# Casting keys, queries and weights inside GpSimd's loads: linear attention with a SiLU feed-forward on one core

## The chip, the core and the metric

The kernel runs on one core of one Trainium2 chip. The metric is device time in microseconds (us); every number called "time" is the median of all executions of that series, slow ones included. An execution over 1.5% above the fastest of the same kernel is called slow, and ratios use fast executions alone. A profile is one execution taken by the hardware profiler; its span is about 2 us shorter than the time of that execution.

Engines: TensorE (PE in profiles; PEld is its weight load), VectorE (DVE), ScalarE (ACT), GpSimd (POOL) and SyncE (SP). SP, GpSimd and ScalarE can issue DMAs. Each engine works through its instructions in order. An instruction that waits holds up all behind it.

## The reference

Decayed linear attention for 4 batches of 8 heads, 768 positions and head size 64, then a feed-forward layer with SiLU, all float32.

```python
for b in range(nb):                                   # blocks of 64 positions
    intra = einsum('bhic,bhjc->bhij', qb, kb) * Dmask # lam ** (i - j), lower triangle
    intra = einsum('bhij,bhjd->bhid', intra, vb)
    inter = einsum('bhid,bhde->bhie', qb * lam_pow, kv_state)
    out[:, :, sl] = intra + inter
    kv_state = lam_block * kv_state + einsum('bhsd,bhse->bhde', kb * rev_pow, vb)
x = out.transpose(0, 2, 1, 3).reshape(3072, 512)
h = x @ w_in                                          # 512 x 2048
return (h * sigmoid(h)) @ w_out                       # 2048 x 512
```

Both kernels write each decay as a product of a power of lam that belongs to the query and one that belongs to the key or value, so the state needs no rescaling.

## The kernel before

All work is a list of operations with durations. A planner in the kernel file puts them into one order, which fixes each engine's order before anything runs. There are 24 chunks of 128 positions. For a chunk, keys and values are loaded as float32, keys are cast to bf16 into a block-diagonal tile (two heads on 128 partitions), that tile is transposed (by TensorE for chunks 0 to 7, by a DMA from SP after that), values are scaled by GpSimd and copied by VectorE into a block-diagonal tile, and queries are scaled by GpSimd. TensorE fills the time between attention steps with feed-forward matmuls of earlier chunks.

The parts that the argument touches (cuts marked `# ...`):

```python
def load_q(b, j):                       # 256 positions, float32, rows of 512 bytes, by SP
    # ...
    nc.sync.dma_start(out=t.tile, in_=q[b, :, 256 * j:256 * j + 256, :].rearrange("h (s t) d -> s h t d", t=2))

def load_seg(src, tag, b, c0, n):       # one piece per head, float32 rows of 256 bytes, by SP
    for hh in range(8):
        # ...
        nc.sync.dma_start(out=t.tile[64 * two:64 * two + 64, :, p, :], in_=r)

def load_w(which, i, n):                # float32 into a staging tile "wt", then a cast
    # ...
    nc.sync.dma_start(out=t.tile.rearrange("p (a b) -> p a b", b=sh[2]), in_=src)
    # ... nc.scalar.activation(dst_j, src_j, AF.Copy)  or  nc.vector.tensor_copy(dst_j, src_j)

def prep_q(b, j, head):                 # decay of queries; chunks from 4 on: GpSimd
    eng = nc.gpsimd if e == "POOL" else nc.vector
    eng.tensor_tensor(tb.tile[:, sl], tf.tile..., tabq[...], op=AL.mult)
    # ... then a transpose by TensorE, or nc.sync.dma_start_transpose

def prep_k(c, src, src_ops, coff, head):
    for h in range(2):
        nc.vector.tensor_copy(kb.tile[hs, :, :, h, :], i)     # float32 -> bf16, block-diagonal
    # ... then a transpose by TensorE (c < 8), or nc.sync.dma_start_transpose

def prep_v(c, src, src_ops, coff, head):
    eng = nc.gpsimd if e == "POOL" else nc.vector
    eng.tensor_tensor(tv.tile, i, t[...].to_broadcast([128, 2, NP, D]), op=AL.mult)
    for h in range(2):
        nc.vector.tensor_copy(vb.tile[hs, :, :, h, :], tv.tile[hs])
```

Rings: two staging tiles each for queries, keys and values, three block-diagonal key tiles, five weight staging tiles. SP issues everything (loads, transposes and stores) except one load of 4 KB.

## Time and profile before

The time was 252.43 us (251.91 to 252.95). The span falls into three stretches:

| stretch, us | TensorE busy, us | what it is |
|---|---|---|
| 0 to 50 | 42.6 of 50 | filling: weights and first chunks arrive, partly matmuls on zeros |
| 50 to 190 | 117.1 of 140 | mixed: attention chunks with feed-forward between |
| 190 to 249 | 55.2 of 59 | dense: the feed-forward of the last eight chunks |

First the page of the kernel before: busy time of the engines, three rows of the map in 40 slices (tenths busy; PEclk is the granted TensorE clock), the chain of work that ended last by engine and by line, and two groups of instructions (line, engine, operation, output <- input, count, busy us, mean ns of one, idle us of the engine ahead of them and what ended most of it).

```profile
span 248.8 us, 4537 instructions
...
PE 214.9 (86%) x1781; PEld 126.3 (51%) x1781; DVE 108.5 (44%) x197; ACT 119.4 (48%) x230; POOL 52.7 (21%) x58
...
PE   6679899969599699566999896995899999999994
...
PEclk9999999997889999997999999999999999999999
DMA  5999999544698998699767989979442001210022
...
PE 48%; DMA 19%; SPq 15%; DVE 9%; issue 3%; POOL 2%; ACT 2%; POOLq 0%; DVEq 0%; ACTq 0%
PE h L633 22%; PE o L656 19%; SPq L303 10%; DMA qf<-in_q_dram 8%; DVE vbd L475 5%; DMA vf<-in_v_dram 3%; DMA wt<-in_moe_w_in_dram 3%; PE op L565 3%; DMA kfh<-in_k_dram 2%; DMA qT<-qb 2%; PE kv L737 2%; DVE sbd L601 1%; POOL vs L468 1%; DMA kf<-in_k_dram 1%; DVE ss L542 1%
...
L468 POOL TENSOR_TENSOR vs<-vf,tab 128x512 bf16<-128x512 f32 x20 | 20.8, 1062 | 86.4 <-DMA vf<-in_v_dram 68.1
L475 DVE COPY vbd<-vs 64x512 bf16<-64x512 bf16 x48 | 29.6, 617 | 19.5 <-POOL vs L468 18.8
...
```

TensorE is busy for 86% of the span, and the map shows the gaps in the middle. SP's issuing makes 15% of the chain ("SPq"). GpSimd's value scaling (L468) sat idle 68.1 us waiting for values to land. The value copy (L475) takes 617 ns in the mean, and stands with 5% in the chain.

The same copy with its spread of durations, from the view of that tile:

```profile
...
L475 DVE COPY vbd<-vs x48: 275/291/2007, 11.6 to 178.1; 64x512 bf16<-64x512 bf16 x48
...
```

A median of 291 ns and a longest of 2007 ns show two kinds of execution: alone, and while something blocks it. Next, who TensorE waited for (total us, times, longest):

```profile
...
PE kv L585 <- POOL vs L468: 8.9, 5, 2.7
PE kv L585 <- DVE sbd L601: 8.8, 5, 3.3
PE sc L536 <- DMA kT<-kbd: 3.0, 1, 3.0
...
PE sc L536 <- DMA qT<-qb: 1.7, 2, 1.1
...
```

The state update ("kv") waits for scaled values and for VectorE's state copies, 8.9 and 8.8 us. Last, the mixed stretch by windows (busy us and instructions in brackets of each engine; then granted clock, mean busy share of the DMA engines, GB/s):

```profile
...
core 0: us, PE busy (x) PEld busy (x) DVE busy (x) ACT busy (x) POOL busy (x), PEclk, DMA share, GB/s
...
50.00:190.00 140.00, 117.13 (x1117) 68.44 (x1114) 78.80 (x140) 63.89 (x131) 37.93 (x29) 0.96 0.82 175
...
```

### The profile page before, as it was taken

Reading aid. Unit: us, or ns where it says so; the run is one execution under the profiler, and the core shown is the slowest. Engines: PE = TensorE matmul, PEld = TensorE weight load, DVE = VectorE, ACT = ScalarE, POOL = GpSimd, SP = SyncE. Lnnn points to the kernel's source line nnn. Section 1 sums busy time; section 2 is a strip of 40 time slices with the busy share of each in tenths; the row PEclk is TensorE's granted clock in tenths of the full one; section 3 lists DMA queues with packets and bytes.
Section 4 is the critical chain, followed back from the end, with each engine's and each line's share of the span. In section 5 each row is a group of like instructions: output and inputs, shape, how many; then the busy total and the mean of one; then the engine's idle time right before and its main releaser. Section 6 shows DMA issues by size and latency. Waiting matters only on the chain.

```text
span 248.8 us, 4537 instructions
## 1 busy us (share of the span) xinstructions
PE 214.9 (86%) x1781; PEld 126.3 (51%) x1781; DVE 108.5 (44%) x197; ACT 119.4 (48%) x230; POOL 52.7 (21%) x58
## 2 busy tenths in 40 slices
PE   6679899969599699566999896995899999999994
PEld 4477776735397386322455352443454444444441
DVE  4884852447286846594177247255740000000000
ACT  2369776723166287421685233654434751177310
POOL 7802100330320910180061005504300000000000
PEclk9999999997889999997999999999999999999999
DMA  5999999544698998699767989979442001210022
GB/s 143 243 281 251 358 383 328 140 125 91 178 243 190 251 216 154 127 285 211 148 161 162 167 192 237 217 156 191 80 122 84 0 0 45 84 42 0 5 82 84
DMA packets 94885, 40.15 MB, mean 161 GB/s; under 512 B 69264, under 2 KB 89744, under 8 KB 94864
## 3 DMA queue, kind: packets, MB, share of 16 engines
q1 hardware_dynamic: 94720, 39.86, 68.1%
q8 instruction: 14, 0.23, 0.4%
q14 instruction: 7, 0.06, 0.1%
q10 hardware_dynamic: 144, 0.00, 0.0%
HBM read 27.27 MB, written 6.29 MB: 135 GB/s over the span
## 4 chain that ended last, share of the span: by engine, by line
PE 48%; DMA 19%; SPq 15%; DVE 9%; issue 3%; POOL 2%; ACT 2%; POOLq 0%; DVEq 0%; ACTq 0%
PE h L633 22%; PE o L656 19%; SPq L303 10%; DMA qf<-in_q_dram 8%; DVE vbd L475 5%; DMA vf<-in_v_dram 3%; DMA wt<-in_moe_w_in_dram 3%; PE op L565 3%; DMA kfh<-in_k_dram 2%; DMA qT<-qb 2%; PE kv L737 2%; DVE sbd L601 1%; POOL vs L468 1%; DMA kf<-in_k_dram 1%; DVE ss L542 1%
## 5 line engine op out<-in xcount | busy, mean ns | idle before, releaser
L633 PE MATMUL h<-x,w_in_bf 128*128 128x256 bf16 (+1 forms) x512 | 92.8, 333 | 0.4 <-ACT g L640 0.4
L656 PE MATMUL o<-w_out_bf,g 128*128 128x512 bf16 x384 | 90.3, 383 | 0.0
L640 ACT ACTIVATE g<-h 128x256 bf16<-128x256 f32 (+1 forms) x128 | 62.0, 490 | 35.8 <-PE h L633 34.0
L633 PEld LDWEIGHTS <-w_in_bf 128*128 128x128 bf16 x512 | 48.9, 99 | 32.9 <-issue 2.2
L656 PEld LDWEIGHTS <-g 128*128 128x128 bf16 x384 | 35.7, 99 | 37.3 <-issue 1.1
L468 POOL TENSOR_TENSOR vs<-vf,tab 128x512 bf16<-128x512 f32 x20 | 20.8, 1062 | 86.4 <-DMA vf<-in_v_dram 68.1
L475 DVE COPY vbd<-vs 64x512 bf16<-64x512 bf16 x48 | 29.6, 617 | 19.5 <-POOL vs L468 18.8
L666 ACT ACTIVATE ob<-o 128x512 f32<-128x512 f32 x24 | 14.3, 597 | 44.6 <-PE o L656 43.5
L371 POOL TENSOR_TENSOR qb<-qf,tab 128x1024 bf16<-128x1024 f32 (+1 forms) x12 | 22.3, 1856 | 34.5 <-DMA qf<-in_q_dram 34.4
L585 PE MATMUL kv<-vs,kbd 128*128 128x64 bf16 x176 | 12.1, 196 | 17.9 <-POOL vs L468 8.9
L599 ACT ACTIVATE sbd<-kv 64x256 bf16<-64x256 f32 x42 | 15.8, 376 | 23.5 <-PE kv L585 18.9
L424 DVE CAST kbd<-kf 64x512 bf16<-64x512 f32 x40 | 19.4, 486 | 16.1 <-DMA kf<-in_k_dram 15.3
L585 PEld LDWEIGHTS <-kbd 128*128 128x128 bf16 x176 | 10.2, 100 | 26.3 <-issue 16.9
L542 DVE TENSOR_TENSOR ss<-sc,mask 128x512 bf16<-128x512 f32 x20 | 13.8, 691 | 16.0 <-PE sc L536 15.6
L601 DVE CAST sbd<-kv 64x256 bf16<-64x256 f32 x38 | 16.0, 422 | 7.9 <-PE kv L585 3.4
L565 PE MATMUL op<-ss,vbd 128*128 128x64 bf16 (+1 forms) x192 | 15.3, 198 | 1.3 <-DVE ss L542 1.0
L615 ACT ACTIVATE x<-op 128x512 bf16<-128x512 f32 x16 | 11.9, 746 | 8.5 <-PE op L565 8.4
L737 PE MATMUL kv<-zt 128*128 128x256 bf16 x69 | 11.3, 319 | 3.7 <-ACT sbd L599 2.1
L565 PE MATMUL op<-qT,sbd 128*128 128x64 bf16 (+1 forms) x160 | 14.4, 196 | 0.0
L565 PEld LDWEIGHTS <-vbd 128*128 128x128 bf16 x192 | 12.8, 99 | 2.5 <-DVE vbd L475 0.6
L565 PEld LDWEIGHTS <-sbd 128*128 128x128 bf16 x160 | 11.5, 99 | 2.7 <-issue 1.3
L536 PE MATMUL sc<-qT,kT 128*128 128x64 bf16 x160 | 7.9, 193 | 4.7 <-DMA kT<-kbd 3.0
(52 smaller groups left out, 94.5 us busy)
## 6 DMA issues: line engine op xcount, KB each, us to landing
qf<-in_q_dram SPq DMA_DIRECT2D x12, 512.0 KB, 5.2
out_dram<-ob SPq DMA_DIRECT2D x24, 256.0 KB, 2.4
wt<-in_moe_w_in_dram SPq DMA_DIRECT2D x8, 512.0 KB, 7.0
wt<-in_moe_w_out_dram SPq DMA_DIRECT2D x4, 1024.0 KB, 10.0
kf<-in_k_dram SPq DMA_DIRECT2D x32, 96.0 KB, 3.0
vf<-in_v_dram SPq DMA_DIRECT2D x32, 96.0 KB, 2.8
kfh<-in_k_dram SPq DMA_DIRECT2D x8, 128.0 KB, 5.6
vfh<-in_v_dram SPq DMA_DIRECT2D x8, 128.0 KB, 5.6
```

The source lines that it names most:

```text
L303: nc.sync.dma_start(out=t.tile[64 * two:64 * two + 64, :, p, :], in_=r)
L371: eng.tensor_tensor(tb.tile[:, sl], tf.tile.rearrange("p h s d -> p s h d")[:, sl], tabq[:, j, sl, :, None].to_broadcast([128, 2 // nn, H, ...
L424: nc.vector.tensor_copy(kb.tile[hs, :, :, h, :], i)
L468: eng.tensor_tensor(tv.tile, i, t[:, :, :, None].to_broadcast([128, 2, NP, D]), op=AL.mult)
L475: nc.vector.tensor_copy(vb.tile[hs, :, :, h, :], tv.tile[hs])
L542: nc.vector.tensor_tensor(sb.tile.rearrange("a s p b -> a (s p) b"), ps.tile.rearrange("a s p b -> a (s p) b"), mask1[:, None].rearrange(" ...
L565: nc.tensor.matmul(o_cols(p, sub), lhsT=l, rhs=r, start=not ovs["started"], stop=i == len(steps) - 1, skip_group_check=True)
L585: nc.tensor.matmul(kvp.tile[:, p, :], lhsT=kb.tile[:, s, p, :, :], rhs=tv.tile[:, s, p, :], start=st, stop=True, skip_group_check=True)
L601: nc.vector.tensor_copy(nb.tile[hs, :, h, :], kvp.tile[hs])
L633: nc.tensor.matmul(hb.tile, lhsT=w_in_bf[:, ko, m * 128:(m + 1) * 128], rhs=xt[g].tile[:, ko, :], start=(ko == 0), stop=(ko == 3))
L640: nc.scalar.activation(gb.tile, hb.tile, AF.Silu)
L656: nc.tensor.matmul(po.tile, lhsT=gts[g, m][0].tile[:, mt * C:(mt + 1) * C], rhs=w_out_bf[:, m, :], start=(m == 0), stop=(m == 15))
```

## The change

The intent is to take the conversion from float32 to bf16 off the compute engines. A DMA issued by GpSimd can cast on its way, so keys (all but those of the first chunk), queries and weights go straight into their final bf16 tiles. The queries' decay is applied when the attention output is copied out of PSUM, where a copy was needed anyway. GpSimd no longer scales anything. It issues loads.

```diff
-GROUPS = [2, 2, 2, 2, 4, 4, 4, 4]
-NHEAD = 4
+GROUPS = [2, 2, 2, 2, 2, 2, 4, 4, 4]
+NHEAD = 2
+NSP = 2
# ... planner: other constants, separate queues, limits for descriptors
-    SLOTS = {"qf": 2, "qb": 2, "qT": 3, "kf": 2, "vf": 2, ..., "kbd": 3, "kT": 3, ..., "ob": 3, "wt": 5, ...}
+    SLOTS = {"qb": 5, "qT": 4, "big": 3, ..., "kseg": 4, "kT": 4, ..., "ob": 7, ...}
# ... queries
-            nc.sync.dma_start(out=t.tile, in_=q[b, :, 256 * j:256 * j + 256, :].rearrange("h (s t) d -> s h t d", t=2))
+            nc.gpsimd.dma_start(out=t.tile[:, jj], in_=q[b, :, C * blk:C * blk + C, :].rearrange("h s d -> s h d"))
# ... keys: eight pieces of a segment, cast into the block-diagonal tile
+                nc.gpsimd.dma_start(out=t.tile[hs, 0:n, p, two, :],
+                                    in_=k[b, hh, 64 * c0:64 * (c0 + n), :].rearrange("(c s) d -> s c d", s=64))
-                    nc.vector.tensor_copy(kb.tile[hs, :, :, h, :], i)
# ... values stay float32; the first two segments from SP, the rest from GpSimd
+                QS[eng].dma_start(out=t.tile[hs, :, p, :], in_=v[b, hh, ...])
# ... weights
-            nc.sync.dma_start(out=t.tile.rearrange("p (a b) -> p a b", b=sh[2]), in_=src)
+        o = load(lambda: nc.gpsimd.dma_start(out=dst, in_=src), ...)
# ... value scaling: VectorE only
-        a = add(f, [("POOL", pool_ns(512))] + ([("DVE", dve_ns(512))] if head else []), ...)
+        a = add(f, ("DVE", dve_ns(512)), ...)
# ... output copy: VectorE only, with the queries' decay
-            if e == "ACT":
-                nc.scalar.activation(dst, ob.tile, AF.Copy)
-            else:
-                nc.vector.tensor_copy(dst, ob.tile)
+            nc.vector.tensor_tensor(xt[g].tile[:, :, C * off:C * off + C], ob.tile, tabo[:, :, C * blk:C * blk + C], op=AL.mult)
```

The planner runs again on the new list, so the order of all engines changes too.

## The prediction

> **What bounds it now.** The profiled span is 248.8 us, in three stretches (busy time by windows):
>
> - 0-20 us, filling: the first FFN matmul starts at 19.8 us (timeline).
> - 20-190 us, mixed: TensorE is busy 145.1 of 170 us. In the view of waits the state update waits 8.9 us for GpSimd's value scaling and 8.8 us for VectorE's state copies; scores wait 4.7 us for transposing DMAs. Granted clock falls to 0.83 in 50-70 and 110-120, badly fed windows.
> - 190-249 us, dense: two FFN groups, four blocks of 64 matmuls at 13.81 us. The change shortens nothing here.
>
> Two causes stand behind the mixed stretch. First, one queue issues every load: in the chain of waits SP issues take 15%, about 0.62 us each, back to back from 49.7 to 76 us; GpSimd's idle time before value scaling is 68 us, waiting for values. Second, VectorE and GpSimd block each other: the value copy takes 275 ns at least, 291 median, 2007 at most, 29.6 us for 48. At the median that would be 14, so an estimated 15.6 us is blocking. The Trainium skill, "SBUF — State Buffer", section "Who interferes with whom", describes an exclusive lock on the shared port; these durations agree.
>
> **What changes.**
>
> - Removed: key casts 24.5 us (VectorE 22.6), weight casts 13.3 us, query scaling 22.3 us and value scaling 21.8 us on GpSimd, the blocking, the weight staging ring.
> - Added to VectorE: value scaling, about 16 us; all 24 output copies with a multiply at about 0.7 us (the mask multiply takes 691 ns), +11 us, while ScalarE loses 11.9; about 9 us of zeroing. VectorE stays near 105 us: not the bound.
> - Moved: issue splits over two queues. GpSimd gets roughly 130 DMAs; at an assumed 0.7-1 us each, 90-130 us. Prefetch deepens (key ring 2 to 4, values 2 to 3, queries 2 to 5 buffers).
> - DMA: reads stay float32. Query rows go from 512 to 256 bytes, 12 thousand packets more on 95 thousand. DMA share is 71% in 50-80 and 66% in 160-190: room there. 0-50 us is saturated (97-100%) and gains little.
>
> **Sum.** First FFN matmul 3 us earlier (no table or multiply ahead of the first scores, a head of two chunks). Of some 23 us of idle TensorE in 50-190, 13 go. Steadier feeding saves 2 us of lowered clock. New waits give back 1. About 17 us of 252.4: **235 us**, range 226 to 245. Faster by over 2%: 0.88; within 2%: 0.08; slower: 0.04.
>
> **What would show it.** Value copies all near 0.29 us; no wait of the state update on GpSimd; SP under 5% of the chain; TensorE busy above 90%; first FFN matmul at 15-18 us; dense blocks still 13.8 us. If VectorE's busy time passes 120 us, or its output copy or value scaling is what TensorE waits for, the moved work was mis-sized.
>
> **What would make it wrong.** The skill, same page, section "SBUF: two separate sides", says GpSimd can't write descriptors while VectorE runs a two-port copy; no run here shows it yet. If a GpSimd issue costs 1.5 us or more, its in-order queue becomes the new single issuer and the gain falls under 6 us. Casting DMAs could move data more slowly than plain ones and delay weights (all needed by about 46 us) and values. A lower granted clock under denser TensorE work would also eat gain.

## The result and the profile after

The time after is 237.44 us (237.16 to 237.73), against 252.43 us before. The ratio is 0.941, with a 95% interval of 0.931 to 0.950. A ratio is the mean time of one kernel's fast runs over that of the other's of the same rounds, so it isn't quite the ratio of the medians quoted. On another chip, with more runs, the same kernel came to 0.934.

The page after, lines that answer those above:

```profile
span 235.3 us, 4708 instructions
...
PE 213.5 (91%) x1871; PEld 133.3 (57%) x1871; DVE 94.3 (40%) x209; ACT 112.0 (48%) x248; POOL 105.9 (45%) x161
...
PE   6699579999999958996999949999999999999993
...
PEclk9999959999999999999999976999999999999999
DMA  7999799796999999999999999999920002100022
...
PE 48%; DMA 36%; POOL 12%; issue 2%; ACT 0%; POOLq 0%; SPq 0%; ACTq 0%
...
L503 DVE COPY vbd<-vs 64x512 bf16<-64x512 bf16 x48 | 16.4, 342 | 0.6
...
```

TensorE is busy for 91% of a span that is 13.5 us shorter. SP's issuing has gone from the chain. In its place stand DMAs with 36% and GpSimd's issuing with 12%. The DMA row reads 9 from about 59 to 170 us, where before it had gaps. Value copies fell from 29.6 to 16.4 us in total, though not all to 0.29 us as predicted (the longest takes 0.67):

```profile
...
L503 DVE COPY vbd<-vs x48: 273/290/669, 9.2 to 177.3; 64x512 bf16<-64x512 bf16 x48
...
```

TensorE's waits and the mixed stretch:

```profile
...
PE sc L557 <- DMA kT<-kseg: 8.9, 5, 3.4
PE kv L605 <- DVE sbd L619: 2.1, 1, 2.1
...
```

```profile
...
50.00:190.00 140.00, 130.77 (x1242) 81.19 (x1239) 58.38 (x114) 70.69 (x165) 74.02 (x107) 0.98 1.37 145
...
```

The 8.9 us for scaled values are gone and the 8.8 us for state copies are 2.1. A new one has come: scores wait 8.9 us for transposing DMAs of keys, which before was 3.0 us. From issue to landing such a transpose took a median of 3.5 us before and 9.5 us after. In all, TensorE's idle time in 50 to 190 us went from 22.9 to 9.2 us. Those 13.6 us are about the whole 13.5 us by which the span fell. The rest nearly cancels: TensorE's idle time in the first 50 us grew from 7.4 to 8.9 us, and its busy time fell from 214.9 to 213.5. The fill didn't shorten (first feed-forward matmul at 19.75 us before, 19.46 after), and blocks of 64 dense matmuls still take 13.81 us.

### The profile page after: what moved, and what is told of

Its sections match the earlier page's. It is cut to its first block, busy times and chain, and to the rows that moved or that the text cites. A ratio compares the mean times of both kernels' runs of the same rounds, so it can differ in the third digit from the quotient of the medians.

```text
span 235.3 us, 4708 instructions
## 1 busy us (share of the span) xinstructions
PE 213.5 (91%) x1871; PEld 133.3 (57%) x1871; DVE 94.3 (40%) x209; ACT 112.0 (48%) x248; POOL 105.9 (45%) x161
## 3 DMA queue, kind: packets, MB, share of 16 engines
q0 software_dynamic: 57056, 15.08, 73.5%
## 4 chain that ended last, share of the span: by engine, by line
PE 48%; DMA 36%; POOL 12%; issue 2%; ACT 0%; POOLq 0%; SPq 0%; ACTq 0%
PE h L652 22%; PE o L678 21%; DMA kT<-kseg 18%; DMA qb<-in_q_dram 15%; DMA kseg<-in_k_dram 3%; POOL kseg L369 3%; POOL qb L312 2%; PE op L585 2%; POOL big L384 2%; POOL w_in_bf L397 2%; PE sc L557 1%; PE kv L605 1%; POOL w_out_bf L397 1%; POOL kbh L344 1%; ACT ob L688 0%
## 5 line engine op out<-in xcount | busy, mean ns | idle before, releaser
L369 POOL DMA_DIRECT2D kseg<-in_k_dram x64 | 41.6, 683 | 41.3 <-DMA qb<-in_q_dram 16.4
L384 POOL DMA_DIRECT2D big<-in_v_dram x48 | 31.7, 679 | 12.8 <-DMA kseg<-in_k_dram 9.5
L617 ACT ACTIVATE sbd<-kv 64x256 bf16<-64x256 f32 x60 | 22.6, 376 | 23.7 <-PE kv L605 21.3
L632 DVE TENSOR_TENSOR x<-op,tabo 128x512 bf16<-128x512 f32 x24 | 16.6, 690 | 29.3 <-PE op L585 29.1
L495 DVE TENSOR_TENSOR vs<-big,tab 128x512 bf16<-128x512 f32 x22 | 14.4, 683 | 23.5 <-DMA big<-in_v_dram 22.9
L312 POOL DMA_DIRECT2D qb<-in_q_dram x24 | 21.6, 920 | 1.1 <-POOLq L783 0.8
L585 PE MATMUL op<-ss,vbd 128*128 128x64 bf16 (+1 forms) x192 | 17.4, 199 | 0.2
L503 DVE COPY vbd<-vs 64x512 bf16<-64x512 bf16 x48 | 16.4, 342 | 0.6
L619 DVE CAST sbd<-kv 64x256 bf16<-64x256 f32 x24 | 10.1, 422 | 12.6 <-PE kv L605 10.5
L557 PEld LDWEIGHTS <-kT 128*128 128x128 bf16 x176 | 7.4, 101 | 12.6 <-DMA kT<-kseg 10.6
L605 PEld LDWEIGHTS <-kseg 128*128 128x128 bf16 x160 | 10.1, 101 | 7.7 <-issue 2.8
L585 PEld LDWEIGHTS <-vbd 128*128 128x128 bf16 x192 | 13.6, 101 | 1.5 <-DVE vbd L503 0.4
```

The costliest lines, as they stand in the source:

```text
L312: nc.gpsimd.dma_start(out=t.tile[:, jj], in_=q[b, :, C * blk:C * blk + C, :].rearrange("h s d -> s h d"))
L369: nc.gpsimd.dma_start(out=t.tile[hs, 0:n, p, two, :], in_=k[b, hh, 64 * c0:64 * (c0 + n), :].rearrange("(c s) d -> s c d", s=64))
L384: QS[eng].dma_start(out=t.tile[hs, :, p, :], in_=v[b, hh, 64 * c0:64 * (c0 + n), :].rearrange("(c s) d -> s c d", s=64))
L557: nc.tensor.matmul(ps.tile[:, sub, p, :], lhsT=tk.tile[:, sub, p, :], rhs=q_cols(p, sub), start=True, stop=True)
L585: nc.tensor.matmul(o_cols(p, sub), lhsT=l, rhs=r, start=not ovs["started"], stop=i == len(steps) - 1, skip_group_check=True)
L617: nc.scalar.activation(nb.tile[hs, :, h, :], kvp.tile[hs], AF.Copy)
```

## The experiments

Twelve kernels ran, four of them built on the kernel before by adding parts, seven on the changed kernel by undoing or moving parts, and one with loads alone. The prediction had named two causes for the mixed stretch: the single issuing queue, and VectorE and GpSimd blocking each other on a port that they share. The rival was that one of the two, or neither, matters, and that the gain comes from the casts that are gone or from loads running further ahead.

Wherever an edit could be made without a new plan, it was: then each engine's order stays, and the text says "same order". "Planned anew" marks the others, whose differences can contain an effect of order.

| kernel | time, us | ratio to before (95% interval) | TensorE busy in 50 to 190 us |
|---|---|---|---|
| before | 252.43 | 1 | 117.1 |
| before_dve | 252.55 | 1.005 (0.996 to 1.014) | 116.7 |
| before_dve_split | 248.21 | 0.988 (0.979 to 0.996) | 124.9 |
| before_dve_split_w | 246.26 | 0.976 (0.965 to 0.987) | 124.2 |
| before_queues | 258.02 | none (one of six runs fast, 252.72) | slow profile |
| after_again (the change, unedited) | 233.51 | 0.934 (0.927 to 0.940) | 131.4 |
| after_lock | 234.01 | 0.927 (0.917 to 0.937) | slow profile |
| after_mix | 240.26 | 0.958 (0.949 to 0.967) | 129.7 |
| after_pet12 | 234.53 | 0.938 (0.933 to 0.944) | 133.9 |
| after_kdve | 257.44 | 1.033 (1.025 to 1.041) | 115.5 |
| after_k2 | 232.94 | 0.933 (0.923 to 0.942) | 131.6 |
| after_zero0 | 233.95 | 0.933 (0.926 to 0.940) | slow profile |

The kernel before was run again in each of four series, at medians of 249.77 to 252.17 us; the first row is the first measurement. The four series ran on four chips, so compare ratios across series, not times. The series are: dma_alone, before_dve, before_dve_split and after_lock; after_again, after_mix, after_pet12 and after_kdve; after_k2, before_dve_split_w and after_zero0; before_queues. What the texts name a call is a series. The ratio of before_dve_split_w rests on two fast executions of four.

### dma_alone: what a casting DMA costs by itself

Loads only, in phases. Between phases VectorE reads and rewrites every tile, so each phase waits for the one ahead. The output is zeros.

```diff
+    seg(nc.sync, False, 0)       # eight key pieces of 128 KB, float32, from SP
+    seg(nc.gpsimd, False, 1)     # the same from GpSimd
+    seg(nc.gpsimd, True, 2)      # the same from GpSimd, cast to bf16
# ... 1 MB of weights and 256 KB of queries likewise; four transposes alone and beside loads
```

> A wrong result on purpose: only loads, phase by phase, with a fence between. First theory (a casting DMA of GpSimd moves data as fast as a plain one, and the longer landings in the changed kernel come from crowding): eight key pieces of 128 KB cast by GpSimd land within 10% of the time of the same pieces uncast from GpSimd, and of SP; a 1 MB weight load likewise; GpSimd's issue stays about 0.66 us beside SP's 0.62. Four transposes alone land in 3 to 5 us each as in the kernel before; behind eight loads of the same queue and beside GpSimd's loads they take 8 us or more. Rival (the cast itself is slow): the cast phase is longer than the uncast one by over 20%, and transposes beside it are no slower than beside plain loads.

The timeline (start us, length us, engine, line, operation; in brackets the idle time ahead and what ended it). Each pair is the issue of a phase and VectorE's first write to the whole landed tile:

```profile
...
14.76 5.48 SPq L55 DMA_DIRECT2D f<-in_k_dram  x8
...
22.73 1.23 DVE L46 COPY f<-f 128x2048 f32<-128x2048 f32 x1 [1.50 <-DMA f<-in_k_dram]
...
24.27 6.87 POOL L55 DMA_DIRECT2D f<-in_k_dram  x8 [23.83 <-DVE f L46]
...
33.52 1.23 DVE L46 COPY f<-f 128x2048 f32<-128x2048 f32 x1 [2.25 <-DMA f<-in_k_dram]
...
36.19 7.13 POOL L55 DMA_DIRECT2D c<-in_k_dram  x8 [5.04 <-DVE c L46]
...
45.28 1.23 DVE L46 COPY c<-c 128x4096 bf16<-128x4096 bf16 x1 [2.25 <-DMA c<-in_k_dram]
...
```

From first issue to first touch: 7.97 us from SP, 9.25 us from GpSimd, 9.09 us from GpSimd with the cast. The cast costs nothing here, with nothing else in flight. Issuing from GpSimd instead of SP costs about 16%, not the under 10% expected. Part of that is VectorE's copies running beside it: GpSimd's issues of plain key pieces took a median of 0.80 us (longest 1.30) there, and value pieces in the last phase, after the copies, 0.72. With 1 MB of weights it was 5.1 us from SP, 7.5 from GpSimd, 6.7 cast; with 256 KB of queries from GpSimd 4.3 us plain and 4.5 cast.

The slower weight load from GpSimd comes with a longer issue:

```profile
...
57.99 2.49 POOL L61 DMA_DIRECT2D wf<-in_moe_w_out_dram  x1 [14.68 <-DVE wf L46]
...
58.75 1.43 DVE L46 COPY tr<-tr 128x1024 bf16<-128x1024 bf16 x4
...
65.49 0.15 DVE L44 COPY tok<-wf 128x1 f32<-128x1 f32 x1 [5.06 <-DMA wf<-in_moe_w_out_dram]
...
```

GpSimd's issue took 2.49 us and ended at 60.48, 0.3 us after VectorE's run of copies at 60.18. The cast weight load (1.89 us) and both query loads (1.53 and 1.86 us) also ended 0.3 to 0.5 us after such a run. In the changed kernel no issue by GpSimd took over 1.02 us. This fits what the Trainium skill says, "SBUF — State Buffer", section "SBUF: two separate sides", by which GpSimd can't write descriptors while a VectorE copy holds the shared port; no phase repeated these loads without copies. It shows under back-to-back copies, but not as a cost in the changed kernel.

Four transposes alone landed 3.1 to 3.3 us after their issues, all within 7.4 us of the first. After eight loads of the same queue all four took 7.6 us. Four of those eight loads had already landed when the first transpose was issued: that part of the expectation missed, and the phase was too weak to test it. Beside GpSimd's loads the four took 5.1 to 15.0 us to land; the median of all twelve transposes is 3.4.

### before_dve: scaling moved to VectorE, so that the port is free

```diff
-                eng = nc.gpsimd if e == "POOL" else nc.vector
+                eng = nc.vector            # in prep_q and in prep_v; the plan stays
```

> The kernel before with query and value scaling computed by VectorE instead of GpSimd, every instruction at its old place in the order. First theory (the shared port is one of the two causes): value copies come to a median of 0.29 us with none over 1 us, the wait of the state update on GpSimd is gone and on VectorE's state copies halved; VectorE busy goes from 108.5 to about 115 us; time 0.97 to 0.99 of before. Rival (only the single issuing queue matters): the copies get faster all the same but TensorE then waits for late values in the same places, and the time is 0.995 to 1.01.

```profile
...
L475 DVE COPY vbd<-vs x48: 274/290/293, 10.3 to 179.3; 64x512 bf16<-64x512 bf16 x48
...
```

```profile
...
50.00:190.00 140.00, 116.65 (x1106) 69.13 (x1121) 83.68 (x170) 63.88 (x132) 0.00 (x0) 0.96 0.79 174
...
```

All 48 value copies are now undisturbed, the longest 293 ns, and 16 us of blocking have vanished. The time is the same, and TensorE is as idle as before. It stops in the same place: at 105.66 us in the kernel before and at 106.02 us here, the state update waits for values that landed late (2.67 and 1.53 us). VectorE is blocked less but works more, 114.3 us against 108.5. So the time that the rival forecast came true.

But this run doesn't show that the blocking was harmless. In the kernel before, TensorE did wait behind blocked copies (VectorE's copies, then TensorE's state update):

```profile
...
108.72 4.34 DVE L475 COPY vbd<-vs 64x512 bf16<-64x512 bf16 x4
...
114.03 0.29 PE L585 MATMUL kv<-vs,kbd 128*128 128x64 bf16 x4 [3.28 <-DVE sbd L601]
...
```

In before_dve, VectorE has two value scalings (0.69 us each) and two query scalings (1.2 us each) between 107 and 115 us, and TensorE waits 1.43 and 1.85 us for state copies there. In all, 25.6 us of scaling (13.4 of values, 12.2 of queries, outside the head) came onto VectorE for 16 us of blocking. What is shown is that this trade is worth nothing. The lock without the added work was not tested.

### before_dve_split: a second queue for values

```diff
-                nc.sync.dma_start(out=t.tile[64 * two:64 * two + 64, :, p, :], in_=r)
+                (nc.gpsimd if tag == "vf" else nc.sync).dma_start(out=t.tile[64 * two:64 * two + 64, :, p, :], in_=r)
```

> As before_dve, and the value pieces are issued by GpSimd (plain, float32, no cast) instead of SP, same order. First theory (single issuing queue is the second cause): values land earlier, waits on values vanish, ratio to before 0.95 to 0.97, at least 1% under before_dve. Rival (the DMA engines and buffers, not the issue, limit): within 0.5% of before_dve.

```profile
...
20.00:50.00 30.00, 24.29 (x203) 17.93 (x203) 14.18 (x27) 17.99 (x34) 2.46 (x4) 0.89 1.08 299
50.00:190.00 140.00, 124.88 (x1186) 75.14 (x1203) 87.73 (x175) 71.53 (x147) 26.08 (x40) 0.98 0.86 174
...
```

In the mixed stretch TensorE gains 8.2 us of busy time against before_dve, and its wait for values is all but gone (0.2 us, from 5.7). The time falls by only 4.3 us between the two medians; 20 to 50 us got worse (24.3 us busy, 27.5 in before_dve). The ratio of 0.988 misses the expected 0.95 to 0.97: the second queue is a real part, but a smaller one than expected.

### before_dve_split_w: weights cast on the way

```diff
-            new(t, [128, 1024 * n], F32, padded=[128, 2048])
-            nc.sync.dma_start(out=t.tile.rearrange("p (a b) -> p a b", b=sh[2]), in_=src)
+            nc.gpsimd.dma_start(out=dst, in_=src)
             def mk(e, j=j):
+                return                     # no cast; the plan stays
```

> The kernel before with scaling on VectorE, values issued by GpSimd, and now the weights cast by GpSimd's DMAs straight into their tiles, the same order (the casts of VectorE and ScalarE, 13 us, drop out; the staging memory stands unused). If the weights' casts and staging were on the critical path: ratio 0.97 or less, against 0.988 without this part. If the first 50 us are bound by the DMA engines anyway: 0.98 to 0.995.

The ratio is 0.976, 0.012 under the step ahead, with intervals that overlap, so this part is worth between nothing and about 2%. The mixed stretch didn't move (124.2 us busy). What moved is 20 to 50 us, back to 27.4 us busy.

This profile also shows what the keys' cast can do where it stands. VectorE waits in front of a cast whose key piece hasn't landed, a mask multiply stands behind that cast, and TensorE waits for the multiply:

```profile
...
76.19 0.42 DVE L424 CAST kbd<-kf 64x512 bf16<-64x512 f32 x1 [4.89 <-DMA kf<-in_k_dram]
...
79.71 0.21 PE L565 MATMUL op<-ss,vbd 128*128 128x64 bf16 x1 [5.47 <-DVE ss L542]
...
```

It is TensorE's longest wait in the mixed stretch, and it is in before_dve_split too (4.71 and 5.38 us).

### before_queues: the changed kernel's queues, but staging and casts kept

Key pieces and later queries now come from GpSimd as well, uncast. SP keeps transposes, stores and the head's loads.

```diff
+            nc.gpsimd.dma_start(out=t.tile[64 * two:64 * two + 64, :, p, :], in_=r)          # keys and values
+            (nc.sync if (b, j) < (0, 2) else nc.gpsimd).dma_start(out=t.tile, in_=q[...])    # queries
```

> As before_dve_split_w, and now the key pieces and the queries (from the third query tile on) are issued by GpSimd too, plain float32, same order: the queues carry what they carry in the changed kernel, transposes and stores on SP, loads on GpSimd, but keys are still staged and cast by VectorE, and rings, order and scaling stay those of before. If separating the loads from transposes that wait for casts is most of what is left: SP's waits no longer delay loads, ratio 0.95 or less. If what is left is the keys' casts themselves, standing in VectorE's order and waiting for late keys, or the new order of the plan: 0.97 to 0.985, with TensorE still waiting behind VectorE.

This was no gain at all: 258.02 us in the median, and the single fast run, 252.72 us, is no better than the kernel before. Both ratios, 0.95 or less and 0.97 to 0.985, missed. The six executions reach from 252.72 to 265.98 us, so the rule for slow runs may be sorting the kernel's own spread here. The profile is of a slow run and is used here only to name the wait that appeared (GpSimd's waits, then TensorE's):

```profile
...
POOL qf L275 <- DVE qb L371: 23.4, 3, 10.6
...
```

```profile
...
PE sc L536 <- DMA qT<-qb: 20.4, 3, 9.8
...
```

GpSimd's queue stands still until VectorE has scaled an old query tile and so freed its staging buffer, and all key and value loads stand behind. The staging of keys and their casts are not what holds it (0.7 us). As far as a slow profile tells, loads on their own queue don't pay while a buffer that they need is freed late by an in-order engine; this run says nothing of the keys' cast.

### after_kdve and after_k2: the keys' cast put back, and its control

after_kdve loads the same key pieces from the same queue as float32 into two staging tiles, and VectorE casts them into two key tiles. after_k2 keeps the casting DMAs and only cuts the key ring from four tiles to two. Both are planned anew.

```diff
# after_kdve
+                nc.gpsimd.dma_start(out=s.tile[hs, :, p, :], in_=k[b, hh, ...])       # float32 staging
+                    nc.vector.tensor_copy(t.tile[hs, i:i + 2, :, two, :], s.tile[hs, i:i + 2])
# after_k2
-             "kseg": 4,
+             "kseg": 2,
```

> The changed kernel with the keys' casting undone: the same pieces from the same queue land as float32 in two staging buffers, and VectorE casts them (about 17 us of casts) into two key tiles (planned anew). If taking the casts off the path from load to transpose is a large part of the gain: ratio above the unedited change by 2% or more, with VectorE's casts in front of transposes and TensorE waiting there. If the gain is from two issuing queues and early loads alone: within 1% of it.

> The control for the run with casts by VectorE: keys still cast by GpSimd's DMAs, but two key tiles in the ring instead of four, no staging (planned anew). If the casts themselves cost the 10% that the run with casts by VectorE lost: ratio within 1.5% of the unedited change (0.934). If it was the ring, the lead that loads have over use: ratio 0.97 or more, with TensorE waiting for transposes of keys or for keys.

The control is as fast as the change, 0.933. With the cast on VectorE the ratio is 1.033, slower than the kernel before. SP's own waits in after_kdve, then TensorE's, then the two mixed stretches, after_kdve first:

```profile
...
SPq L483 <- DVE kseg L379: 37.3, 5, 14.7
...
```

```profile
...
PE sc L567 <- DMA kT<-kseg: 14.2, 5, 6.1
PE sc L567 <- DMA qT<-qb: 8.4, 2, 4.4
...
```

```profile
...
50.00:190.00 140.00, 115.52 (x1064) 73.75 (x1081) 65.14 (x129) 59.71 (x145) 74.95 (x107) 0.91 1.24 155
...
```

```profile
...
50.00:190.00 140.00, 131.63 (x1218) 81.19 (x1239) 57.24 (x112) 71.52 (x167) 74.20 (x107) 0.99 1.32 144
...
```

SP waits 37.3 us in five transposes for casts by VectorE. No wait of SP on VectorE stands among the ten largest of after_k2. TensorE waits 22.6 us for transposes of keys and queries, and loses 16 us of busy time against after_k2. Over the whole span TensorE is idle 16.8 us longer and busy 6.7 us longer, at a mean granted clock of 0.931 against 0.978.

It would be easy to put this down to casts that stand in VectorE's way. The traces say that this is the smaller part. Both kernels issue the same eight key pieces from GpSimd, from 63.0 to 68.5 us in after_kdve and from 62.8 to 68.4 in after_k2. When they landed (the tile's view for 58 to 70 us; after_kdve first, with VectorE's first cast of them, then after_k2):

```profile
...
L370 POOL DMA_DIRECT2D kf<-in_k_dram x8: 683/688/757, 63.0 to 67.8; - x8
...
DMA to landing us min/median/max: 4.3/9.2/14.6
...
81.65 0.42 DVE L379 CAST kseg<-kf 64x512 bf16<-64x512 f32 x1 [10.45 <-DMA kf<-in_k_dram]
...
```

```profile
...
L369 POOL DMA_DIRECT2D kseg<-in_k_dram x8: 787/816/854, 62.8 to 67.5; - x8
...
DMA to landing us min/median/max: 4.2/6.5/7.2
...
```

The cast pieces had all landed by 74.8 us, the plain ones by 82.4. SP issued the first transpose at 74.94 and at 82.93 us, and TensorE's longest wait, 6.1 us for a transposed key, ends at 89.64. The cast itself took about half a microsecond of that. The next waits for keys (2.3 and 5.1 us) are for transposes that had been issued but took 11 and 16 us to land, and one for queries (4.1 us) for a transpose whose issue SP held until a key piece had landed. Casts do come late in VectorE's order at 141 and 160 us, 8 to 9 us after their pieces landed; behind the second of these, at most the last wait of TensorE (4.4 us, for queries) follows. Plain pieces don't always land later: the slowest of each group of eight in the mixed stretch took 14.6, 8.9, 16.6, 8.6 and 8.7 us plain, and 7.2, 12.5, 11.6, 12.8 and 11.1 cast. Why the first and the third group were so late, when alone plain and cast take the same time (dma_alone), was not tested. Both runs are planned anew, so part of the difference can also be the plan's order.

### after_lock and after_mix: value scaling back on GpSimd

```diff
-            eng = nc.gpsimd if e == "POOL" else nc.vector
+            eng = nc.vector if head else nc.gpsimd          # after_lock: 22 of 24 chunks
+            eng = nc.vector if c < 12 else nc.gpsimd        # after_mix: chunks 12 to 23
```

> The changed kernel with the scaling of values back on GpSimd (22 of 24), every instruction at its place in the order. First theory: value copies of up to 2 us and the wait of the state update return, GpSimd's DMA issues are delayed behind the multiplies, ratio to before 0.97 to 1.0 (the changed kernel has 0.94). Rival (the gain came from deeper prefetch and two queues, the lock is hidden by them): ratio 0.94 to 0.955.

> The changed kernel with value scaling of chunks 12 to 23 on GpSimd, of 0 to 11 on VectorE, every instruction at its place in the order. The run with all of it on GpSimd lost 7.5 us in one stall at 86 to 93 us, where two multiplies stood behind DMA issues[...], and was still no slower than the change. New theory (the change is limited by how fast transposing DMAs of keys land beside GpSimd's loads; multiplies between the issues thin the loads out): the 7.5 us stall is gone, the wait on transposes in 100 to 160 us falls from 5.2 us to under 2, and the ratio is 0.01 to 0.03 below the unedited change of this call. Rival (placing the multiply is neutral, the earlier difference was the chip): within 0.5% of it. Old theory (the shared port costs): 1% above or more.

In after_lock the long copies came back, as expected:

```profile
...
L503 DVE COPY vbd<-vs x48: 221/292/1718, 9.1 to 176.2; 64x512 bf16<-64x512 bf16 x48
...
```

The time did not follow: 0.927, against 0.934 of the unedited change in another series, intervals overlapping. That is no loss, and it isn't shown to be a gain. The trade of before_dve comes out even from the other side too: VectorE is blocked again, but scales less.

The theory that multiplies between the issues thin out the loads and help the transposes fell at once: after_mix was slower than the change, 0.958. In its profile two multiplies stood behind key loads that GpSimd was issuing until 133.20 us. TensorE was idle for 3.66 us ahead of its state update at 134.31 us; the profile names a key load as the releaser, but the first multiply ended just then. In the profile of after_lock (a slow run) the same pattern cost 7.5 us at another place. Where GpSimd both issues and computes, it depends on the place in its order whether this costs something.

### after_pet12: transposing chunks 8 to 11 by TensorE

```diff
-NPET = 8
+NPET = 12
```

> The changed kernel with keys and queries of chunks 8 to 11 transposed by TensorE instead of DMAs (the order is planned anew). If late transposes are the new limit: the waits on transposes in 80 to 97 us (3.8 us) go, TensorE pays about 2.6 us more of its own work, and later transposes find the queue freer; ratio within 1% of the unedited change, or below it by up to 1%. If transposes are late only because keys themselves land late: no gain, and TensorE waits for key loads in their place, ratio above it by 1% or more.

0.938 against 0.934: no gain and no clear loss. The wait of scores on transposes of keys fell from 7.3 us in the unedited change of that series to 1.5 us, a wait on one transpose of queries came (3.4 us), and TensorE was busy 3.9 us longer. Late transposes are a real wait, but buying them off with TensorE's own time is about even.

### after_zero0: zeroing out of the way of the fill

```diff
+            nc.scalar.activation(t[:, i]..., zt[...], AF.Copy)       # first key tile: zeroed by ScalarE
+                 at=[0.0, 20000.0, 34000.0, 44000.0][n]              # the other three: later, by VectorE
```

> The changed kernel with the zeroing of the first key tile on ScalarE (8 pieces) and that of the other three held back to 20, 34 and 44 us on VectorE. If zeroing in the fill delays the start (GpSimd waited 4.8 us for it before its first key loads; 4.1 us of it stood in front of a state copy at 24 to 28 us): GpSimd's wait for zeroing is under 1 us, TensorE's wait of 2.1 us for that state copy is gone, ratio 0.01 to 0.02 below the unedited change, about 0.92. If the fill is bound by the DMA engines: within 0.5% of it.

0.933 against 0.934: nothing. The waits did go (GpSimd's wait for zeroing, 4.8 us, is no longer among its waits), but GpSimd then waited longer for other loads to land (7.7 us on pieces of the first weights, 2.7 before the edit), and the first feed-forward matmul came at 20.1 us. The profile is of a slow run. That fits a fill set by what the DMA engines deliver, but no run shows it directly.

### after_again: the yardstick

The changed kernel, unedited.

> The changed kernel, unedited, as the yardstick of this call: ratio to before 0.935 to 0.95, and TensorE's wait of scores on the transposing DMAs of keys of 6 to 12 us again. If it comes to 0.93 or less, the run with value scaling on GpSimd was not faster than the change, only measured on another chip.

0.934, slightly under the expected 0.935, with 7.3 us of waits on transposes of keys. No edit of the changed kernel beat it by more than the interval.

## Why the prediction was right or wrong

**The total.** Predicted 235 us in 226 to 245; measured 237.44. Partly this is luck: of the sum's four terms (fill 3, mixed stretch 13, clock 2, new waits -1) only the 13 held, and it was right in size with reasons that were half wrong.

**Idle TensorE in 50 to 190 us: 13 of about 23 us go.** Measured 13.6 of 22.9. The size was right.

**"Two causes stand behind the mixed stretch."** Half of it failed. The blocking between VectorE and GpSimd was read correctly from the durations of the copies (16 us of 29.6), and the Trainium skill, "SBUF — State Buffer", section "Who interferes with whom", explains them rightly: without GpSimd's multiplies all 48 copies took under 0.3 us. But before_dve removed the blocking and the time stayed, after_lock brought it back and the time stayed. The step that failed is to count the blocking as a gain without its price: the scaling went onto the same VectorE, 25.6 us of it in before_dve, in front of the same waits of TensorE. The blocked copies did stand in the chain (5%), so it isn't shown that they were harmless, only that this way of removing them brings nothing. The single queue was a cause, but giving the values a queue of their own is by itself worth about 1% (0.988, interval 0.979 to 0.996).

**What stood in its place.** The prediction listed the removed casts as busy time of engines that weren't the bound, and gave them no share of the gain. The runs show that casting keys inside the load matters: with it and a ring of two key tiles 0.933, with plain loads, VectorE's casts and the same ring 1.033. Two ways are seen in the traces, and their shares are not measured. First, a cast that waits for a late piece holds up all work behind it on VectorE: 5.5 us of TensorE's time at one place of before_dve_split_w. In the kernel before, VectorE stood 15.3 us in front of such casts, in the changed kernel no such wait is left. Second, and larger in after_kdve, two groups of plain float32 pieces landed late (up to 14.6 us against 7.2 for cast pieces issued at the same time), and transposes with them; the cause of that is open. before_queues doesn't decide here: what held its loads was the staging of queries.

**First feed-forward matmul 3 us earlier.** Failed: 19.46 us against 19.75. VectorE is busy 17.4 of the first 20 us, against 14.0 before, with zeroing, masks and value scaling among it. Taking the zeroing out didn't help, so that isn't the whole reason.

**2 us from a steadier clock.** Failed: the mean granted clock was 0.977 before and 0.971 after, with dips elsewhere (0.72 in 30 to 40 us, 0.76 in 140 to 150).

**"New waits give back 1."** Too small: the waits of scores on transposing DMAs of keys alone grew from 3.0 to 8.9 us. "Room there" in the DMA engines was wrong: the mean busy share in 50 to 190 us went from 0.82 to 1.37 (overlapping packets count double), and a transpose lands in 9.5 us, not 3.5. These waits are inside the 13.6 us net.

**VectorE near 105 us.** It is 94.3. One part of the difference is that the new plan moved state copies to ScalarE: on VectorE they fell from 16.0 to 10.1 us, on ScalarE they rose from 15.8 to 22.6. Zeroing the key tiles took 8.4. VectorE isn't the bound, as predicted.

**GpSimd's issuing.** 0.61 to 1.02 us each and 105.9 us in all, inside the predicted 90 to 130. The feared 1.5 us didn't come.

**Casting DMAs slow?** No: alone 9.09 against 9.25 us for eight pieces, and beside other traffic neither kind is always the later (after_kdve, after_k2).

**Still open.** How much of the remaining difference between before_dve_split_w (0.976) and the change (0.934) is the keys' cast, how much the queries' decay moved to the output copy, and how much the new order of the plan. The first is shown to be large in the changed kernel's setting, where undoing it loses more than the whole gain, so the parts don't simply add; the others were not undone alone. The deeper rings of queries and values were not either.

## What to carry to other kernels

A conversion that costs an engine little time can still cost much if it stands between a load and the work behind it: look at what an in-order engine holds up while it waits, not at its busy share. Then look at when the data landed, before the engine is blamed: in after_kdve TensorE's longest stall began with a late load. Long durations that a conflict explains are worth nothing until a run without the conflict is faster; here 16 us of blocking were traded for other work on the same engine. When loads get a queue of their own and run ahead, expect just-in-time transfers, such as transposes, to land later.

## What the Trainium skill lacked or had wrong

- "DMA: Bandwidth & Descriptors" says that casting needs GpSimd's queue but gives no rate for it. Measured alone: eight 128 KB key pieces 9.09 us cast and 9.25 us plain; 1 MB of weights 6.7 and 7.5 us (with issues of 1.89 and 2.49 us in them). Beside other traffic the slowest of eight key pieces took 7.2 to 12.8 us to land cast (after_k2) and 8.6 to 16.6 us plain (after_kdve).
- The same page, section "Issuing engines are not separate DMA queues", calls the issue time that several issuing engines save "usually small relative to the DMA itself". With pieces of 64 to 128 KB it was 0.62 us of about 3 us to landing, and a second issuing engine took 8.2 us of idle TensorE out of the mixed stretch (though only 4.3 us out of the time). With the move the values' loads also no longer stood behind SP's transposes; the run doesn't separate the two.
- The same page, section "Queues, rings and completion order", describes how a DMA engine goes round its queues packet by packet, but not what that does to a transfer needed at once: transposes beside GpSimd's loads landed in a median of 9.5 us in place of 3.5, and in up to 15.0 us in dma_alone.
- No page says how casting DMAs show up as packets. GpSimd's queue in the changed kernel, most of its values' loads plain among them, has 57,056 packets for 15.08 MB, about 264 bytes each; with plain loads in before_dve_split 2,432 packets for 5.25 MB, about 2.2 KB each. Yet in dma_alone cast and plain took about the same time.
- "SBUF — State Buffer", section "SBUF: two separate sides": the descriptor lock was seen with back-to-back copies (issues of 1.53 to 2.49 us that ended 0.3 to 0.5 us after the copies). The page names the copies that lock GpSimd out and describes a single stalled load, but not what a kernel with mixed work loses; with the changed kernel's mixture no issue took over 1.02 us.
